# Window attention and two MLPs on one core: products with v of two pairs in one run, v stationary from the third window, and another model of VectorE's hold in the list schedule

## The chip, the core and the metric

The kernel runs on 1 core of one Trainium2 chip. The metric is the device time of one execution in microseconds; the median of 3 runs before the change is 892.06 us (892.01 to 892.25). One further execution was profiled, and the rows below are from it. Engines are TensorE (PE; PEld is its weight load), VectorE (DVE), ScalarE (ACT), GpSimd (POOL) and SyncE (SP), whose queue issues nearly all DMAs.

## The reference

Attention over 4 batches, 8 heads, 576 tokens, head size 64, with a window: heads 0 to 3 see the last 32 tokens, heads 4 to 7 every fourth of the last 128. Then two MLPs on the 2304 tokens of width 512 and inner width 2048.

```python
rel = pos[:, None] - pos[None, :]
mask_plain = (rel >= 0) & (rel < 32)
mask_dil = (rel >= 0) & (rel < 128) & (rel % 4 == 0)
scores = np.where(mask, q @ k.T / np.sqrt(64), -1e9)
attn = np.exp(scores - scores.max(-1)); attn = attn / (attn.sum(-1) + 1e-9)
x = (attn @ v)                                   # heads side by side: 2304 x 512
h = x @ w_in1; x = np.maximum(0.01 * h, h) @ w_out1
h = x @ w_in2; out = (np.maximum(h, 0) + np.log1p(np.exp(-abs(h)))) @ w_out2
```

## The kernel before, in words

**Attention.** The tokens are cut into 8 windows of 288 (half a batch each; `w` is 0 to 7). In each window four pairs of heads (`p` 0 to 3) are worked on: pairs 0 and 1 are plain, pairs 2 and 3 dilated. For a pair TensorE forms scores with keys on the partitions and queries along the free axis (L661 for dilated pairs, L674 for plain ones, from the third window on), VectorE adds the mask (L682, L689), GpSimd takes the maximum over the partitions (`rowmax`, L699, a `partition_all_reduce`), VectorE subtracts it (L703), ScalarE takes the exponential (L706). What comes then has two forms.

- *Scores stationary* (`pv`, L724): the exponentials are the stationary operand, v with a column of ones moves. Each row's sum comes out as column 65; ScalarE and VectorE make the reciprocal and scale (`inv_sum`, `inv`: L734, L740, L741), and TensorE transposes the result (`xT`, L750). A dilated pair has its products in two halves, each with a PSUM bank of its own.
- *v stationary* ("turned"; `pv_late`, L760): v is the stationary operand, 64 columns wide, one half of the array's columns for each of the two heads; the exponentials move, and the result is transposed already. The sums come from a second `partition_all_reduce` on GpSimd (`sums`, L768); VectorE spreads them by transposes (`spread`, L776), adds 1e-9, takes reciprocals and transposes back (`recip`, L781 to L784), and scales (`norm`, L788).

In both forms ScalarE rounds the result to a high part (`x_hi`, L807) and VectorE subtracts for the low part (`x_lo`, L811). These go into one of two rooms for x, and are what the first MLP's products read; each pair makes a quarter of the width of x. Before the change a pair is turned if `w >= 3 and (dilated or p == 0 or w > 3)`: 19 pairs.

**First MLP.** Eight blocks of tokens (256, 256, 352 and then 288 wide), 16 slices of the inner width each: 12 products for h (L833), then on ScalarE and VectorE the activation and its split in two parts (L849, L854, L858), then 12 products into y (L876). These main products fill TensorE; attention for later windows runs between them. VectorE and ScalarE also turn the weights of both MLPs from their raw words into high and low parts (L321 to L381).

**Second MLP.** It starts when the last block is done, from about 500 us on, and has no attention beside it (L1017, L1078, L1090).

**What sets the order.** All work is written as operations with an engine, an estimated cost, dependences, buffers that it takes and gives back, and a due time. `run_schedule` simulates the engines on these costs, takes at each step the ready operation with the earliest due time, and puts out the program in that order. On the chip every engine runs its instructions in that order, and waits only for data and buffers. Due times go back from each block's first product: the last low part of pair `p` is due `11 * (3 - p)` us ahead of that of pair 3 (`STAG`). Buffers that matter here: 2 score tiles (`s`), 1 tile for maxima and sums (`mx`), 2 tiles for reciprocals (`xn`), 2 PSUM banks for attention (`at`), 2 tiles each for k, q and v.

The schedule also models that VectorE runs slower or not at all while GpSimd runs a `partition_all_reduce`. An operation with a `lock` has its simulated end put off; one with a small `lock` is also ranked 6 us later (`WAIT`) while the hold lasts. Before the change the hold lasts for the whole GpSimd operation from 75 us on, and the VectorE operation goes on at 0.33 or 0.7 of its speed; ahead of 75 us it lasts 1.2 us and stops it.

Of the kernel before, what the change touches and what calls it, by code (L numbers as in the profile page):

```python
# [11 lines left out]
F32 = mybir.dt.float32  # L12
# [14 lines left out]
def kernel(  # L27
# [58 lines left out]
    TURN = 3  # L86
# [7 lines left out]
    class Op:  # L94
        def __init__(self, eng, cost, fn, *args, deps=(), order=(), acq=(), rel=(),
                     target=None, margin=0.0, start=0.0, lib=None, slack=0.0, lock=0.0, optional=False, hold=0.0, lead=None, shy=False):
# [11 lines left out]
    def run_schedule(slots):  # L108
# [64 lines left out]
        running = {}  # L173

        def slowed(start, work, rate):
            beside = locked - start
            return start + (work / rate if work <= rate * beside else beside + work - rate * beside)

# [5 lines left out]
        while True:  # L184
# [17 lines left out]
            for e in engines:  # L202
# [3 lines left out]
                for o in pools[e]:  # L206
                    if ready_at[o] <= now + 1e-9 and all(free[a] >= o.acq.count(a) for a in o.acq):
                        rank = (ready_at[o] if e == "bw" else o.prio) + (HOLD if switch(o) else 0.0) + (WAIT if 0.0 < o.lock < 0.5 and now < locked else 0.0), o.n
# [26 lines left out]
                if best.lib == "reduce":  # L235
                    locked = best.end if now > LOCK_FROM else now + LOCKED
                    beside = running.get("dve")
                    if now > LOCK_FROM and beside is not None and beside.lock and beside.end > now:
                        beside.end = slowed(now, beside.end - now, beside.lock)
                        busy["dve"] = beside.end - TRAIL["dve"]  # L240
                        heapq.heappush(events, beside.end)
                        heapq.heappush(events, busy["dve"])
                if best.lock and now < locked:
                    best.end = slowed(now, best.cost, best.lock) if now > LOCK_FROM else locked + best.cost
                running[e] = best
# [239 lines left out]
    class Pair:  # L485
        def __init__(self, w, p):
# [8 lines left out]
            self.turned = w >= TURN and (self.dil or p == 0 or w > TURN)  # L495
# [258 lines left out]
        def pv_late(self):  # L754
            m, kn = self.m, self.kn
            self.xn = att.tile([P, T1], F32, tag="xn", name="xn")
# [15 lines left out]

# [39 lines left out]


# [324 lines left out]
    NSPIN, LOCKED, LOCK, LOCK_FROM, SLACK0, SLACK, HOLDS = 150, 1.2, 0.33, 75.0, 0.3, 1.0, 1.5  # L1138
    LOCKT = 0.7
# [53 lines left out]
    for w in range(NW):  # L1193
# [3 lines left out]
        for p in range(NPAIR):  # L1197
# [58 lines left out]
            else:  # L1256
                nk = a.s0 + T1 - a.klo
                tk = Op("dve", dve(nk) if not dil or a.first else 2 * dve(nk), a.trans_k, deps=[lk] + old_kq, rel=["kr"], lock=LOCKT, **m)
                tq = [Op("dve", (1.0 if turned else 1.2) if dil else 0.48, a.trans_q, deps=[lq] + (old_kq if dil else []),
                         rel=["qr"] if dil else [], lock=LOCKT, **m)]  # L1260
# [56 lines left out]
            for b in blocks:  # L1317
                xready.setdefault(b, []).append(xl)
# [310 lines left out]
```

## Time and profile before

| | |
|---|---|
| median of 3 runs | 892.06 us |
| profiled execution | 890.93 us, its span 889.1 us |
| TensorE busy | 878.9 us, 99% of the span |
| VectorE busy | 654.1 us, 74% |
| ScalarE busy | 399.1 us, 45% |
| GpSimd busy | 146.8 us, 17% |
| maxima of 24 pairs (L699) | mean 2.08 us |
| sums of 19 pairs (L768) | mean 3.74 us |

Busy time of TensorE is the union of its products, whose ends are modelled: products are pipelined, so what one costs is read from the distance of the starts. Time in the rows is counted from the start of the span.

### The profile page before, as it was taken

The page shows a single profiled execution, that of the slowest core. Times are in us where ns is not written, and L with a number is a line of the kernel's source. Part 1 is how long each engine was busy: PE and PEld are TensorE (multiplying, and loading weights), DVE is VectorE, ACT ScalarE, POOL GpSimd, SP SyncE. Part 2 cuts the span into 40 slices and gives each one's busy share as a digit, 9 for nine tenths or more (in the row PEclk, how much of TensorE's full clock was granted, in tenths as well). Part 3 has the DMA queues.
Part 4 walks back from the last instruction along what each step waited for, and adds up shares of the span by engine and source line. Part 5 has one row for each costly group of instructions (what it writes and reads, how often), then busy time and mean ns, then how long its engine had stood idle before and what let it go on. Part 6 is the DMA issues. An engine that isn't in the chain of part 4 may idle for free.

```text
span 889.1 us, 16856 instructions
## 1 busy us (share of the span) xinstructions
PE 878.9 (99%) x6621; PEld 822.2 (92%) x6621; DVE 654.1 (74%) x1166; ACT 399.1 (45%) x780; POOL 146.8 (17%) x71
## 2 busy tenths in 40 slices
PE   9989999999999999999999999999999999999998
PEld 6889999999999999999999999989888898888886
DVE  5999986897897887978944766857765775576553
ACT  5878765345444443444445644324322432243231
POOL 6500120332452433435400000000000000000000
PEclk9999999999999999999999999999999999999999
DMA  9887235664644626435259578333533443334332
GB/s 236 240 261 261 49 83 190 173 180 144 168 123 135 167 65 181 99 107 153 77 167 304 149 227 252 116 101 114 163 122 97 142 146 109 102 112 149 95 95 96
DMA packets 150736, 132.19 MB, mean 149 GB/s; under 512 B 92480, under 2 KB 131200, under 8 KB 150656
## 3 DMA queue, kind: packets, MB, share of 16 engines
q1 hardware_dynamic: 149632, 129.96, 49.1%
q10 hardware_dynamic: 1024, 1.15, 0.5%
q8 instruction: 52, 0.85, 0.4%
q14 instruction: 28, 0.23, 0.1%
HBM read 104.86 MB, written 26.21 MB: 147 GB/s over the span
## 4 chain that ended last, share of the span: by engine, by line
PE 94%; DMA 2%; DVE 2%; ACT 1%; issue 1%; SPq 0%; DVEq 0%; ACTq 0%
PE yp L876 23%; PE yo L1090 23%; PE h L833 23%; PE h L1017 18%; PE hp L1078 3%; DMA raw<-in_moe_w_out_dram 2%; PE pv L760 1%; PE sc L661 1%; PE sc L674 1%; PE pv L724 1%; DVE cf L330 0%; DVE w L381 0%; PE xt L750 0%; DVE cf L339 0%; DVE xn L741 0%
## 5 line engine op out<-in xcount | busy, mean ns | idle before, releaser
L876 PE MATMUL yp<-gh,w 128*128 128x288 f32 (+2 forms) x1024 | 229.1, 299 | 0.0
L833 PE MATMUL h<-xh,w 128*128 128x288 f32 (+2 forms) x1024 | 226.7, 297 | 0.0
L1090 PE MATMUL yo<-wo,w 128*128 128x512 f32 x864 | 222.8, 395 | 0.0
L1017 PEld LDWEIGHTS h<-tr,w 128*128 128x128 f32 x1344 | 174.3, 188 | 11.1
L1090 PEld LDWEIGHTS yo<-wo,w 128*128 128x128 f32 x864 | 152.5, 188 | 27.1
L1017 PE MATMUL h<-tr,w 128*128 128x256 f32 x1344 | 176.7, 279 | 0.0
L876 PEld LDWEIGHTS yp<-gh,w 128*128 128x128 f32 x1024 | 171.3, 188 | 1.9
L833 PEld LDWEIGHTS h<-xh,w 128*128 128x128 f32 x1024 | 171.1, 188 | 1.1
L833 PE MATMUL h<-xl,w 128*128 128x288 f32 (+2 forms) x512 | 151.2, 295 | 0.4 <-DVE xl L811 0.4
L876 PE MATMUL yp<-gl,w 128*128 128x288 f32 (+2 forms) x512 | 150.9, 295 | 0.0
L1055 ACT ACTIVATE ex<-ex 128x512 f32<-128x512 f32 x72 | 45.5, 632 | 159.9 <-DVE ex L1052 158.4
L849 ACT ACTIVATE hc<-h 128x288 f32<-128x288 f32 (+2 forms) x128 | 52.0, 406 | 118.2 <-PE h L833 112.5
L833 PEld LDWEIGHTS h<-xl,w 128*128 128x128 f32 x512 | 96.2, 188 | 0.9 <-DVE xl L811 0.9
L876 PEld LDWEIGHTS yp<-gl,w 128*128 128x128 f32 x512 | 96.2, 188 | 0.1
L858 DVE TENSOR_TENSOR gl<-hc,gh 128x288 fp32r<-128x288 f32 (+2 forms) x128 | 73.9, 578 | 28.7 <-ACT gh L854 27.8
L699 POOL PARTITION_ALL_REDUCE mx<-s x24 | 50.0, 2083 | 243.1 <-DVE s L682 186.8
L768 POOL PARTITION_ALL_REDUCE sm<-s x19 | 71.1, 3740 | 31.8 <-ACT s L706 27.5
L1058 DVE SCALAR_TENSOR_TENSOR ex<-hs,ex 128x512 f32<-128x512 f32 x64 | 44.3, 692 | 35.9 <-ACT ex L1055 35.6
L1063 ACT ACTIVATE w<-ex 128x512 fp32r<-128x512 f32 x72 | 45.3, 629 | 32.8 <-DVE ex L1058 32.8
L321 ACT ACTIVATE cf<-raw 128x512 f32<-128x512 f32 (+1 forms) x48 | 39.9, 830 | 40.7 <-DMA raw<-in_moe_w_out_dram 15.4
L854 ACT ACTIVATE gh<-hc 128x288 fp32r<-128x288 f32 (+2 forms) x128 | 56.6, 442 | 2.9
L1067 DVE TENSOR_TENSOR w<-ex,w 128x512 fp32r<-128x512 f32 x72 | 49.7, 691 | 10.9 <-ACT w L1063 6.2
(113 smaller groups left out, 966.6 us busy)
## 6 DMA issues: line engine op xcount, KB each, us to landing
wo<-w2o SPq DMA_DIRECT2D x80, 512.0 KB, 3.6
raw<-in_moe_w_in_dram SPq DMA_DIRECT2D x32, 512.0 KB, 6.5
raw<-in_moe_w_out_dram SPq DMA_DIRECT2D x32, 512.0 KB, 4.2
w2o<-cf SPq DMA_DIRECT2D x16, 512.0 KB, 3.1
w2a<-cf SPq DMA_DIRECT2D x8, 512.0 KB, 2.6
w2s<-cs SPq DMA_DIRECT2D x8, 512.0 KB
w<-w2a SPq DMA_DIRECT2D x8, 512.0 KB
out_dram<-o SPq DMA_DIRECT2D x28, 128.0 KB, 3.0
```

Source lines behind the costliest of these rows:

```text
L699: nc.gpsimd.partition_all_reduce(self.mx, self.sf, channels=P, reduce_op=bass_isa.ReduceOp.max)
L768: nc.gpsimd.partition_all_reduce(self.sm, self.sf, channels=P, reduce_op=bass_isa.ReduceOp.add)
L833: nc.tensor.matmul(out=h, lhsT=a[:, c, :], rhs=b_[:, c, :], start=(c == 0 and a is whi and b_ is xh), stop=(c == NC - 1 and a is wlo))
L849: nc.scalar.activation(out=hc, in_=hbank.pop(s), func=AF.Prelu, alpha=0.01)
L854: nc.scalar.activation(out=gh, in_=hcopy[s], func=AF.Copy)
L858: eng.tensor_sub(out=gl, in0=hcopy.pop(s), in1=gparts[s][0].bitcast(F32))
L876: nc.tensor.matmul(out=ybank[e][:, o:o + n], lhsT=a[:, e * P:(e + 1) * P], rhs=b_, start=(f == 0 and n == unit_len[u] and a is whi and b_ ...
L1017: nc.tensor.matmul(out=bank[m, b][:, half], lhsT=w[:, a, kb * P:(kb + 1) * P], rhs=t[:, b_, kb], start=(kb == 0 and a + b_ == 0), stop=(kb ...
L1055: nc.scalar.activation(out=self.ex, in_=self.ex, func=AF.Softplus)
L1063: nc.scalar.activation(out=self.gh, in_=self.ex, func=AF.Copy)
L1067: nc.vector.tensor_sub(out=self.gl, in0=self.ex, in1=self.gh.bitcast(F32))
L1090: nc.tensor.matmul(out=obank[c, t], lhsT=a, rhs=b_, start=(opens and n == 0), stop=(closes and n == 2))
```

## The change

- `TURN` goes from 3 to 2, and the rule to `w >= TURN and (dilated or w > TURN)`: the two dilated pairs of the third window and the second plain pair of the fourth become turned, 22 in all.
- Two turned pairs (p 0 and 1, or 2 and 3) share one run on TensorE, `pv_two`. It depends on both pairs' reciprocals and v, takes both `at` banks, and gives both score tiles back at its end. The scalings, `x_hi` and `x_lo` of both pairs come behind it. `xn` is taken at the spreading of the sums, no longer ahead of the products.
- In the schedule's model, a `lock` is now yes or no. A GpSimd reduction holds VectorE for 1.2 us from its start if its cost is under 3 us (a maximum), else for 2.45 us (a sum); a VectorE operation with a lock that starts in that time ends at the hold's end plus its own cost. The transposes (`trans_k`, `trans_q`, `spread`) have no lock any more.

```diff
-    TURN = 3
+    TURN = 2
...
-            self.turned = w >= TURN and (self.dil or p == 0 or w > TURN)
+            self.turned = w >= TURN and (self.dil or w > TURN)
...
                 if best.lib == "reduce":
-                    locked = best.end if now > LOCK_FROM else now + LOCKED
-                    beside = running.get("dve")
-                    if now > LOCK_FROM and beside is not None and beside.lock and beside.end > now:
-                        beside.end = slowed(now, beside.end - now, beside.lock)
...
+                    locked = now + (LOCKED if best.cost < 3.0 else LOCKEDS)
                 if best.lock and now < locked:
-                    best.end = slowed(now, best.cost, best.lock) if now > LOCK_FROM else locked + best.cost
+                    best.end = locked + best.cost
...
+    def pv_two(a, b):
+        a.pv_late()
+        b.pv_late()
...
             if turned:
-                pv = a.o_pv = Op("pe", 0.84, a.pv_late, deps=x + [lv],
-                                 order=[prev(1, "o_pv")], acq=["at", "xn"], **ms)
                 sm = Op("pool", 3.6, a.sums, deps=x, acq=[tag_mx], lib="reduce", **m)
-                t = Op("dve", 2 * dve(288), a.spread, deps=[sm, pv], rel=[tag_mx, tag_s], lock=LOCKT, **m)
-                t = Op("dve", 0.9, a.recip, deps=[t], acq=["rd"], rel=["rd"], lock=LOCKT, **m)
-                xt = Op("dve", dve(288, True), a.norm, deps=[t], rel=["at"], hold=HOLDS, **m)
+                t = Op("dve", 2 * dve(288), a.spread, deps=[sm], acq=["xn"], rel=[tag_mx], **m)
+                t = Op("dve", 0.9, a.recip, deps=[t], acq=["rd"], rel=["rd"], lock=True, **m)
+                a.late, a.lands, xt = t, lv, None
+                if p % 2:
+                    b_ = pairs[-1]
+                    a.o_pv = b_.o_pv = Op("pe", 2 * 0.84 - 0.3, pv_two, b_, a, deps=[t, b_.late, lv, b_.lands],
+                                          order=[pairs[-2].o_pv], acq=["at", "at"], rel=[tag_s, tag_s], **ms)
+                    xt = [Op("dve", dve(288, True), c_.norm, deps=[a.o_pv], rel=["at"], hold=HOLDS, **m) for c_ in (b_, a)]
...
+            for c_, xt_ in ([(a, xt)] if not turned else zip((pairs[-1], a), xt) if p % 2 else ()):
...
+                xh = c_.o_xh = Op("act", act(288, not turned), c_.x_hi, deps=[xt_], order=[pairs[at_ - 1].o_xh if at_ else None],
...
+                xl = Op("dve", dve(288, not turned), c_.x_lo, deps=[xh], rel=[c_.room(c_.p)[1] if not turned else "xn"], lock=turned,
+                        target=tau(first_slot) - 0.5 - stag * (NPAIR - 1 - c_.p), **m)
```

## Rows read from the trace of the kernel before

**Rows 1.** Busy time by stretches: start:end, length, then each engine; PEclk is the granted clock
```profile
58.00:880.00 822.00, 822.00 (x5974) 775.22 (x5973) 606.99 (x1085) 355.89 (x688) 121.06 (x43) 1.00 0.48 143
85.00:210.00 125.00, 125.00 (x1008) 122.79 (x1007) 106.44 (x188) 68.56 (x136) 28.71 (x11) 1.00 0.48 130
210.00:450.00 240.00, 240.00 (x1952) 233.73 (x1951) 200.17 (x364) 104.97 (x222) 92.35 (x32) 1.00 0.47 130
880.00:889.10 9.10, 4.85 (x21) 3.56 (x19) 1.38 (x2) 1.20 (x2) 0.00 (x0) 1.00 0.32 116
```

**Rows 2.** Timeline of TensorE (start, length, instruction, count): a dilated pair, v stationary
```profile
312.92 0.29 PE L833 MATMUL h<-xh,w 128*128 128x288 f32 x1
313.15 0.72 PE L760 MATMUL pv<-s,v 104*64 104x72 f32 x16
...
314.04 0.30 PE L876 MATMUL yp<-gl,w 128*128 128x288 f32 x1
314.17 0.30 PE L876 MATMUL yp<-gh,w 128*128 128x288 f32 x1
```

**Rows 3.** The same: a plain pair, v stationary
```profile
301.50 0.29 PE L833 MATMUL h<-xh,w 128*128 128x288 f32 x1
301.72 0.72 PE L760 MATMUL pv<-s,v 128*64 128x96 f32 x12
...
302.60 0.29 PE L876 MATMUL yp<-gl,w 128*128 128x288 f32 x1
```

**Rows 4.** The same: a dilated pair, scores stationary, and its transposes
```profile
119.72 0.28 PE L876 MATMUL yp<-gh,w 128*128 128x256 f32 x1
119.83 1.20 PE L724 MATMUL pv<-v,s 104*72 104x65 f32 x16
...
121.04 0.28 PE L833 MATMUL h<-xl,w 128*128 128x256 f32 x1
...
126.03 0.28 PE L833 MATMUL h<-xh,w 128*128 128x256 f32 x1
126.15 0.41 PE L750 MATMUL xt<-ident,xn 72*128 72x72 f32 x4
...
126.57 0.28 PE L876 MATMUL yp<-gl,w 128*128 128x256 f32 x1
126.69 0.28 PE L876 MATMUL yp<-gh,w 128*128 128x256 f32 x1
```

**Rows 5.** The same: a plain pair, scores stationary
```profile
109.00 0.28 PE L876 MATMUL yp<-gh,w 128*128 128x256 f32 x1
109.12 1.15 PE L724 MATMUL pv<-v,s 128*96 128x65 f32 x12
...
110.28 0.28 PE L833 MATMUL h<-xl,w 128*128 128x256 f32 x1
```

**Rows 6.** Groups of TensorE by shape: count, busy us, mean ns of one
```profile
L760 PE MATMUL pv<-s,v 104*64 104x72 f32 x160 | 7.2, 232 | 0.0
```

**Rows 7.** Timeline of GpSimd: a sum
```profile
164.68 3.60 POOL L768 PARTITION_ALL_REDUCE sm<-s  x1 [2.11 <-ACT s L706]
```

**Rows 8.** Groups of VectorE by line, 85 to 450 us: count, busy us, mean ns
```profile
L776 DVE STREAM_TRANSPOSE xn<-sm 64x288 f32<-64x288 f32 x38 | 17.8, 468 | 2.4 <-POOL sm L768 2.2
L781 DVE TENSOR_SCALAR rd<-xn 128x9 f32<-128x9 f32 x19 | 11.1, 585 | 0.0
L784 DVE STREAM_TRANSPOSE xn<-rd 128x288 f32<-128x288 f32 x19 | 9.1, 478 | 0.6
```

**Rows 9.** Timeline of VectorE: the same shift, alone and beside that sum
```profile
128.91 0.42 DVE L326 TENSOR_SCALAR cp<-cf 128x512 uint32<-128x512 uint32 x1
...
164.80 2.69 DVE L326 TENSOR_SCALAR cp<-cf 128x512 uint32<-128x512 uint32 x1
```

**Rows 10.** Timeline of VectorE: the last low part ahead of the fifth block
```profile
272.65 0.70 DVE L811 TENSOR_TENSOR xl<-xn,xh 128x288 fp32r<-128x288 f32 x1 [0.24 <-ACT xh L807]
```

**Rows 11.** Timeline of TensorE: the first product of the fifth block
```profile
273.69 0.29 PE L833 MATMUL h<-xh,w 128*128 128x288 f32 x1
```

More of the change, by code (lines that the diff above doesn't have):

```diff
@@ L95, in __init__ @@
         def __init__(self, eng, cost, fn, *args, deps=(), order=(), acq=(), rel=(),
-                     target=None, margin=0.0, start=0.0, lib=None, slack=0.0, lock=0.0, optional=False, hold=0.0, lead=None, shy=False):
+                     target=None, margin=0.0, start=0.0, lib=None, slack=0.0, lock=False, optional=False, hold=0.0, lead=None, shy=False):
             self.eng, self.cost, self.fn, self.args = eng, cost, fn, args
@@ L171, in begins @@
                 coming[u.eng].append(u)
[L173 to L177, printed above, removed]
         result = []
@@ L207, in run_schedule @@
                     if ready_at[o] <= now + 1e-9 and all(free[a] >= o.acq.count(a) for a in o.acq):
-                        rank = (ready_at[o] if e == "bw" else o.prio) + (HOLD if switch(o) else 0.0) + (WAIT if 0.0 < o.lock < 0.5 and now < locked else 0.0), o.n
+                        rank = (ready_at[o] if e == "bw" else o.prio) + (HOLD if switch(o) else 0.0) + (WAIT if o.lock and now < locked else 0.0), o.n
                         if best is None or rank < best_rank:
@@ L771, in spread @@
         def spread(self):
+            self.xn = att.tile([P, T1], F32, tag="xn", name="xn")
             src = self.sm.rearrange("p (t j m) -> p t j m", t=self.nt, j=2)
@@ L1257 @@
                 nk = a.s0 + T1 - a.klo
-                tk = Op("dve", dve(nk) if not dil or a.first else 2 * dve(nk), a.trans_k, deps=[lk] + old_kq, rel=["kr"], lock=LOCKT, **m)
+                tk = Op("dve", dve(nk) if not dil or a.first else 2 * dve(nk), a.trans_k, deps=[lk] + old_kq, rel=["kr"], **m)
                 tq = [Op("dve", (1.0 if turned else 1.2) if dil else 0.48, a.trans_q, deps=[lq] + (old_kq if dil else []),
-                         rel=["qr"] if dil else [], lock=LOCKT, **m)]
+                         rel=["qr"] if dil else [], **m)]
             tag_s, tag_mx = ("es", "emx") if early else ("s", "mx")
@@ L1304 @@
                                 rel=[a.room(half if dil else p)[1], "rd"], **m))
-            room = [f"x{u % 2}" for u in rooms] if p == 0 else []
+            rooms_x = [f"x{u % 2}" for u in rooms]
+            room = rooms_x if p == 0 else []
             if not turned:
@@ L1346 @@
         lw = Op("act", act(n), a.low, order=[o], **m)
-        o = Op("dve", dve2(n), a.shift, deps=[o], acq=["cp"], lock=LOCK, **m)
-        o = Op("dve", dve(n), a.join, deps=[o], rel=["cp"], lock=LOCK, **m)
-        o = Op("dve", dve(n), a.add, deps=[o, lw], rel=["raw"] if layer else [], lock=LOCK, **m)
+        o = Op("dve", dve2(n), a.shift, deps=[o], acq=["cp"], lock=True, **m)
+        o = Op("dve", dve(n), a.join, deps=[o], rel=["cp"], lock=True, **m)
+        o = Op("dve", dve(n), a.add, deps=[o, lw], rel=["raw"] if layer else [], lock=True, **m)
         if layer == 0:
             o = Op("act", act(n), a.split_hi, deps=[o], **m)
-            wready[0, f] = Op("dve", dve(n), a.split_lo, deps=[o], rel=["cf"], lock=LOCK, **m)
+            wready[0, f] = Op("dve", dve(n), a.split_lo, deps=[o], rel=["cf"], lock=True, **m)
         else:
```

30 lines of the change are left out of this document (11 added, 19 removed).

## The prediction

> **What bounds the kernel now.** I read the busy time by stretches first. From 58 to 880 us TensorE is busy for all 822.00 us at the full granted clock; only the last 9.1 us, where the result drains, have holes (4.85 busy) [rows 1]. The reader is to see in that table that no other engine fills its stretch: between 85 and 210 us VectorE has 106.44 of 125 us and GpSimd 28.71, and TensorE all of it. So in this region the end moves with TensorE alone: a microsecond of its work that goes is a microsecond off the end, as long as nothing that it needs comes late. Attention for a window of 288 tokens runs between the two products of earlier tokens. Everything that the change touches lies between 85 and 450 us.
>
> **Prices of one run, from the order of TensorE's work.** Then I read the timeline around the attention runs. I take the start of the last main product ahead of a run and the start of the second main product behind it, and subtract two usual steps. What is left is what the run costs. A step is 0.134 us for 288 columns (314.04 to 314.17 [rows 2], rounded there).
> - Dilated pair, v stationary: 314.04 - 312.92 - 0.27 = 0.85 us [rows 2].
> - Plain pair, v stationary: 302.60 - 301.50 - 0.27 = 0.83 [rows 3].
> - Dilated pair, scores stationary (a step of 256 columns: 126.57 to 126.69): products 121.04 - 119.72 - 0.23 = 1.09, transposes behind them 126.57 - 126.03 - 0.23 = 0.31, together 1.40 [rows 4].
> - Plain pair, scores stationary: products 110.28 - 109.00 - 0.23 = 1.05 [rows 5]; its transposes have three instructions where the dilated have four, estimated at 0.28 from those; together 1.33.
>
> How much of the 0.85 is paid per run, and how much per product? Sixteen instructions take 0.72 us [rows 2], the last alone about 0.23 (mean 232 ns [rows 6]), so the step is (0.72 - 0.23) / 15 = 0.033 us and sixteen steps are 0.52. The remaining 0.33 us is at the two edges: the first product starts 0.23 us behind the last main one instead of 0.13, and the rest is lost behind the run. The run with scores stationary has hardly any edge: (1.20 - 0.23) / 15 is 0.065, sixteen steps are 1.03 of a cost of 1.09 [rows 4]. That run is also two pieces of the program, one for each half of the pair on a PSUM bank of its own, so pieces in a row need not pay at their joint. The edge belongs to the tile of 64 columns, which is entered and left.
>
> **The change part by part.**
> (1) *Two pairs in one run.* 19 pairs keep v stationary before; after, 22 do: both dilated pairs of the third window and all four pairs of the five windows behind it. They make 11 runs, where each alone would make 22. Each joint saves one edge: 11 x 0.33 = 3.6 us. No row shows two such runs in succession. The bounds are 0 (the second pair's first products start as a run's first do) and 11 x 0.35 = 3.9 (the edge, and the wait of a second entry). I take 0.33, since the two pairs of a run have the same tile shape.
> (2) *Three more pairs with v stationary.* Two dilated: 2 x (1.40 - 0.85) = 1.1 us. One plain, the second of the fourth window: 1.33 - 0.83 = 0.5.
> (3) *What these three add elsewhere.* Three sums on GpSimd at 3.60 us [rows 7], and on VectorE per pair two transposes of 0.47, an addition of 0.585 (mean, holds included) and a transpose of 0.48 [rows 8], some 2 us, in place of the old reciprocals and scalings. Cover: VectorE's 18.6 idle us and GpSimd's 96 in 85 to 210 us [rows 1]. Counted as nothing; with that cover gone it costs at most 3 x 2 us.
> (4) *The products moved behind both reciprocals.* On the chip the run waits for the exponentials, v and two PSUM banks, not for the reciprocals; only its place in TensorE's order moves. What waits behind it: both score tiles (there are two) come free only then, so the next pair's scores come later; and both v tiles, so the next v loads come later, and with them the q, k and weight loads behind them in SP's one queue. The chain of two pairs through the single tile for maxima and sums is some 20 us (estimate: two sums at 3.60, two maxima and the VectorE steps between them). The time for it is 30 us: 210 to 450 us hold 32 GpSimd operations, two for a pair, so 16 pairs in 240 us [rows 1]. Counted as nothing. With that cover gone the next scores would wait for the difference; the PSUM banks themselves are held for a shorter time, as the scaling follows at once.
> (5) *VectorE's hold in the list schedule.* No instruction is added, only the order changes. A sum starts on GpSimd at 164.68 and runs 3.60 us [rows 7]; the shift on VectorE that starts at 164.80 takes 2.69 us to 167.49, where the same shape takes 0.42 alone [rows 9]. So it was held until 167.07, 2.4 us into the sum, and then ran at its usual speed while the sum went on. That is the new model's phase of 2.45; the old one slowed such operations to a third over the whole sum. I expect the list's times to come nearer to the chip's. Bounds: no gain is to be had, since no wait is left to remove in 58 to 880 us; the loss through a worse order is in the rivals. Value 0.
> The Trainium skill's page "SBUF — State Buffer", section "Who interferes with whom", says that whoever issues first keeps the shared ports for its whole instruction and the other engine is fully blocked. By it the shift would have ended at 168.28 + 0.42 = 168.70; the trace has 167.49, so it agrees about the blocking and not about its length.
>
> Sum: 3.6 + 1.1 + 0.5 = 5.2 us less on TensorE, all on the path. The profiled execution took 890.93 us (span 889.1 and 1.83 around it), so 885.7. The median of the runs shown is 1.13 above the profiled one: **886.9 us**.
>
> **Rivals.**
> *A. The last pair is late for its block (slower).* Ahead of the fifth block of tokens the last low part of the attention output starts at 272.65 and takes 0.70 [rows 10]; the block's first product starts at 273.69 [rows 11] and needs that part, its last quarter, eight products later, at about 274.8. The lead is 1.4 us. Between the last reciprocal and that low part the new order puts a run of 0.85 + 0.52 = 1.37 us, a second scaling (some 0.45) and a second low part (0.70), with handovers of about 0.24 as in that row some 3.2 us. If pairs start when they start now, TensorE stands 3.2 - 1.4 = 1.8 us; at six windows 10.8, less 5.2, is 5.6 us more: 897.7. It decides from a loss of 0.9 us per window, a last low part 2.3 us nearer to its block. Against it: the shared run takes its due time from its earlier pair, which the schedule places 11 us ahead of the later one, so the later pair's scores, maximum and sum are ranked that much earlier than now. Chance 0.10.
> *B. The joint saves nothing.* For it: no row of two such runs. Then 1.6 us remain: 890.4. Chance 0.06.
> *C. VectorE becomes the bound* early in 85 to 210 us, where it still splits the weights of the first products, with the third window's pairs pulled ahead; TensorE then waits for weights for as long as it gained: about 892. Against it: 18.6 us idle there. Chance 0.05.
> *D. The gain comes, less 1 to 2 us of new waits* in the reshuffled order: about 888.3. For it: VectorE has under a sixth of its time left. Chance 0.12.
> *E. VectorE is held for the whole sum*, so the new list is too early by 3.60 - 2.4 = 1.2 us for a held operation; at two windows with a lead as small as that of the fifth block this is 2.4 us: 889.3. The row of the shift speaks against it. Chance 0.03. (This is the rule of the Trainium skill's page named in part 5.)
>
> **How the numbers follow.** The forecast has 0.64, its own range 886.2 to 887.7 (joints at 0.28 to 0.35, waits of up to half a microsecond). 0.2% of the median is 1.8 us, about what a measurement of this kernel can tell from no change. Faster: the forecast, D and E, 0.79. Same: B and C, 0.11. Slower: A, 0.10. The range goes from 885.8 (joints at 0.35, and handovers of TensorE that shrink a little) to 890.4, which takes in D, E and B and leaves out C and A.
>
> **What would show it.** Right: 11 runs of 24 to 32 instructions at line L760, each costing about 1.35 us by the same subtraction; no transposes at L750 for the third window's dilated pairs and the fourth window; 22 sums on GpSimd; TensorE busy without a hole from 58 to 875 us. A joint at which the second pair's first product starts 0.2 us or more behind the first pair's last shows B. Waits of a block's first product for a low part show A, waits for split weights C. Operations of VectorE begun at a sum's start that end some 2.4 us later plus their own time agree with the new list's phase; ends behind the sum show E. The forecast is wrong if TensorE's holes between 58 and 875 us add up to more than 1 us.

## The result, and the profile after

The changed kernel takes 898.27 us (median of 4 runs, 897.61 to 898.68); the kernel before, beside it, 892.03 (890.93 to 892.25). The ratio is 1.0072 [1.0054, 1.0089]: slower by 6.2 us, where 5.2 us less were forecast. The profiled execution took 898.44 us, its span 896.7. A few executions took some 14 us more than the others of the same kernel; every change of time below leaves them out. Line numbers in a row are those of its own kernel: L823 and L866 here are L833 and L876 of the kernel before, L746 and L754 are L760 and L768.

The busy time by stretches, columns as in [rows 1]; 85 to 147 us is the stretch in which the third window's pairs now have sums:

```profile
58.00:880.00 822.00, 815.55 (x5938) 769.09 (x5937) 608.17 (x1091) 352.73 (x682) 133.40 (x46) 1.00 0.47 142
85.00:147.00 62.00, 60.94 (x548) 59.74 (x548) 57.61 (x93) 38.63 (x71) 17.56 (x6) 1.00 0.28 68
210.00:450.00 240.00, 234.71 (x1918) 227.80 (x1915) 194.78 (x363) 103.14 (x221) 92.45 (x32) 0.99 0.48 132
```
and the same 62 us of the kernel before:
```profile
85.00:147.00 62.00, 62.00 (x558) 61.38 (x557) 52.30 (x93) 38.34 (x75) 9.27 (x4) 1.00 0.35 87
```

TensorE had no hole from 58 to 880 us in [rows 1]; now it has 6.45 us of them, where the prediction took more than 1 us as the sign that it is wrong. And holes are not all: products that run at the lower clock count as busy (rows below). VectorE goes from 52.30 to 57.61 busy us of 62 in the early stretch, so that 4.4 us of it are idle; over 85 to 210 us it still has 14.3 idle (106.44 to 110.67 busy of 125).

The runs on TensorE cost what was forecast. The timeline around one shared run, for [rows 2, 3]:

```profile
331.86 0.29 PE L866 MATMUL yp<-gh,w 128*128 128x288 f32 x1
332.08 1.22 PE L746 MATMUL pv<-s,v 104*64 104x72 f32 x32
333.23 0.40 PE L823 MATMUL h<-xh,w 128*128 128x288 f32 x1
333.47 0.29 PE L823 MATMUL h<-xl,w 128*128 128x288 f32 x1
```

333.47 - 331.86 - 0.27 is 1.34 us for two pairs; the eleven runs lie at 1.33 to 1.35. Summed by the same subtraction, attention's runs cost 47.1 us before and 41.8 after, waits left out: 5.3 less.

The rest is waits. I add up, from 57 to 860 us, by how much each main product starts later behind the one ahead than its usual step, and by how much each attention run costs more than its price: 0.2 us before, 12.0 after. Span against span: 11.8 of waits, less 5.3 of work, plus 0.7 by which the first block's first product starts later (39.84 instead of 39.14 us; run 6, in the same order, has 38.96), is 7.2 of the 7.6 us. The 12.0 us lie in five places: 1.9 at 101 to 109 us, 0.4 near 199.5, 4.6 at the start of the fourth block (214.5 to 222.6), 2.4 a little later (229.8 to 235.6), most of it where that block's first products into y wait for the copies of the third block's y, and 2.8 in four waits for `gl`, the low part that VectorE makes for the products into y.

**The fourth block**, the dearest. TensorE's timeline:

```profile
216.78 0.29 PE L823 MATMUL h<-xh,w 128*128 128x288 f32 x1
219.03 0.40 PE L823 MATMUL h<-xh,w 128*128 128x288 f32 x1 [1.96 <-ACT xh L793]
219.72 0.61 PE L823 MATMUL h<-xl,w 128*128 128x288 f32 x1 [0.29 <-DVE xl L797]
...
221.08 0.49 PE L866 MATMUL yp<-gh,w 128*128 128x352 f32 x1
221.38 0.49 PE L866 MATMUL yp<-gl,w 128*128 128x352 f32 x1
```
ScalarE, VectorE and SP's queue beside it:
```profile
217.74 0.66 ACT L308 ACTIVATE cf<-raw 128x512 f32<-128x512 f32 x1 [3.23 <-DMA w2o<-cf]
218.30 1.28 ACT L793 ACTIVATE xh<-xn 128x288 fp32r<-128x288 f32 x2
...
214.31 0.82 DVE L774 TENSOR_TENSOR xn<-pv,xn 128x288 f32<-128x288 f32 x2
...
219.01 1.27 DVE L797 TENSOR_TENSOR xl<-xn,xh 128x288 fp32r<-128x288 f32 x2 [0.16 <-ACT xh L793]
...
211.14 0.33 SPq L357 DMA_DIRECT2D w2o<-cf  x1
211.56 4.38 SPq L546 DMA_DIRECT2D v<-in_v_dram  x6
```

`x_hi` needs only the scaled output, which VectorE has ready at 215.1 (L774). But ahead of it in ScalarE's order stands the first step of a weight conversion (L308), and that waits for the buffer `cf`, from which a store is still going out. The store is issued at 211.14, with two raw loads ahead of it and six loads of v behind, and its end releases ScalarE at 217.74: 6.6 us. The list has the store issued at 204.57 and landed at 207.07, 5.1 us ahead of the block's first product (212.19 in the list); on the chip it lands 1.7 us behind that product (216.01). Of this change of 6.8 us, 4.1 are the landing and 2.7 that the issue is late against TensorE. The first half of `x_hi` then comes some 2 us late. Behind the stop TensorE has a granted clock of 0.55 over 3.8 us, so the lower of its two levels (1.2 GHz) for most of that stretch, and 352-column products start some 0.3 us apart (221.08, 221.38) where 0.16 is usual:

```profile
215.00:216.70 1.70, 1.70 (x17) 1.54 (x17) 0.72 (x2) 0.00 (x0) 0.00 (x0) 1.00 0.95 307
219.10:222.90 3.80, 3.51 (x13) 3.30 (x14) 3.80 (x8) 1.89 (x5) 0.00 (x0) 0.55 0.34 119
223.00:229.00 6.00, 6.00 (x47) 5.68 (x47) 4.14 (x11) 2.05 (x5) 3.29 (x1) 1.00 0.88 235
```

**The waits for `gl`.** GpSimd, VectorE and TensorE around the first of the four, for [rows 7, 9]:

```profile
268.19 3.70 POOL L754 PARTITION_ALL_REDUCE sm<-s  x1 [3.60 <-ACT s L693]
...
267.75 0.69 DVE L317 SCALAR_TENSOR_TENSOR cf<-cf,cp 128x512 uint32<-128x512 uint32 x1
268.48 2.90 DVE L326 CUSTOM_DVE_ANT_0 cf<-raw,cf 128x1024 uint16<-128x1024 uint16 x1
271.30 0.44 DVE L848 TENSOR_TENSOR gl<-hc,gh 128x288 fp32r<-128x288 f32 x1
...
271.80 0.40 PE L866 MATMUL yp<-gl,w 128*128 128x288 f32 x1 [0.49 <-DVE gl L848]
```

A sum starts at 268.19. The operation begun at 267.75 ends in its usual time (268.44); the next, of a line that takes 0.69 us undisturbed, takes 2.90 to 271.38: 0.69 behind 270.69, which is 2.5 us into the sum. So the phase is as part 5 read it from the shift, and as the new model has it. What the model can't know is on which side of a sum's start an operation falls: in these rows 0.3 us (268.48 against 268.19) make 2.2 us.

### The profile page after: what moved, and what is told of

Same layout as the page of the kernel before. It is cut to its first block, busy times and chain, and to the rows that moved or that the text cites. A ratio compares the mean times of both kernels' runs of the same rounds, so it can differ in the third digit from the quotient of the medians.

```text
span 896.7 us, 16821 instructions
## 1 busy us (share of the span) xinstructions
PE 878.6 (98%) x6610; PEld 821.1 (92%) x6610; DVE 656.5 (73%) x1174; ACT 397.1 (44%) x775; POOL 159.0 (18%) x74
## 4 chain that ended last, share of the span: by engine, by line
PE 55%; POOL 1%; DVE 1%; SPq 1%; DMA 1%; issue 0%; ACT 0%; POOLq 0%
PE yo L1080 22%; PE h L1007 18%; PE yp L866 6%; PE h L823 6%; PE hp L1068 2%; SPq L529 1%; DMA raw<-in_moe_w_in_dram 1%; POOL mx L686 0%; POOL sm L754 0%; PE pv L746 0%; DVE rd L767 0%; PE sc L648 0%; DVE s L676 0%; DVE xn L762 0%; PE sc L661 0%
## 5 line engine op out<-in xcount | busy, mean ns | idle before, releaser
L866 PE MATMUL yp<-gh,w 128*128 128x288 f32 (+2 forms) x1024 | 229.2, 298 | 1.7 <-DVE ys L884 1.1
L823 PE MATMUL h<-xh,w 128*128 128x288 f32 (+2 forms) x1024 | 227.5, 297 | 2.0 <-ACT xh L793 2.0
L866 PEld LDWEIGHTS yp<-gh,w 128*128 128x128 f32 x1024 | 172.2, 188 | 3.9 <-DVE ys L884 1.6
L823 PEld LDWEIGHTS h<-xh,w 128*128 128x128 f32 x1024 | 171.5, 188 | 3.2 <-ACT xh L793 2.2
L866 PE MATMUL yp<-gl,w 128*128 128x288 f32 (+2 forms) x512 | 151.8, 296 | 1.4 <-DVE gl L848 1.3
L823 PE MATMUL h<-xl,w 128*128 128x288 f32 (+2 forms) x512 | 151.6, 296 | 0.7 <-DVE xl L797 0.7
L848 DVE TENSOR_TENSOR gl<-hc,gh 128x288 fp32r<-128x288 f32 (+2 forms) x128 | 76.3, 597 | 35.8 <-ACT gh L844 32.2
L866 PEld LDWEIGHTS yp<-gl,w 128*128 128x128 f32 x512 | 96.5, 188 | 2.7 <-DVE gl L848 2.6
L823 PEld LDWEIGHTS h<-xl,w 128*128 128x128 f32 x512 | 96.4, 188 | 1.4 <-DVE xl L797 1.4
L754 POOL PARTITION_ALL_REDUCE sm<-s x22 | 82.8, 3764 | 46.9 <-ACT s L693 31.7
L308 ACT ACTIVATE cf<-raw 128x512 f32<-128x512 f32 (+1 forms) x48 | 39.8, 829 | 65.1 <-DMA raw<-in_moe_w_in_dram 25.4
L1057 DVE TENSOR_TENSOR w<-ex,w 128x512 fp32r<-128x512 f32 x72 | 49.7, 691 | 10.3 <-ACT w L1053 5.5
```

Source lines behind the costliest of these rows:

```text
L754: nc.gpsimd.partition_all_reduce(self.sm, self.sf, channels=P, reduce_op=bass_isa.ReduceOp.add)
L823: nc.tensor.matmul(out=h, lhsT=a[:, c, :], rhs=b_[:, c, :], start=(c == 0 and a is whi and b_ is xh), stop=(c == NC - 1 and a is wlo))
L848: eng.tensor_sub(out=gl, in0=hcopy.pop(s), in1=gparts[s][0].bitcast(F32))
L866: nc.tensor.matmul(out=ybank[e][:, o:o + n], lhsT=a[:, e * P:(e + 1) * P], rhs=b_, start=(f == 0 and n == unit_len[u] and a is whi and b_ ...
L1057: nc.vector.tensor_sub(out=self.gl, in0=self.ex, in1=self.gh.bitcast(F32))
```

## The experiments

These explanations of the 12 us of waits stood against each other: the new hold model puts out a worse order (H in the expectations); pairing crowds buffers and queues (P); the third window's turn falls on a VectorE that has no room (W); or any order other than that of before meets such waits by chance (N). A further one, that one instruction waits in a queue ahead of the fourth block (Q), came from the rows above; M is the thought that a list whose stores land later is better anywhere.

Each change of the time below is of medians, against the kernel before, run beside it on the same chip. *Work* is what the prices in the prediction take from TensorE; *waits* are counted in that run's profile as above, so in one execution.

| run | change of time, us | ratio, interval | work | waits |
|---|---|---|---|---|
| the kernel after | +6.2 | 1.0072 [1.0054, 1.0089] | -5.2 | 12.0 |
| 1 after, old hold | +6.9 | 1.0070 [1.0045, 1.0094] | -5.2 | 13.5 |
| 2 before, new hold | +3.6 | 1.0038 [1.0023, 1.0053] | 0 | 3.8 |
| 3 after, third window as before | +0.6 | 1.0005 [0.9995, 1.0014] | -3.8 | 5.4 |
| 4 before, three more pairs turned | +3.1 | 1.0036 [1.0023, 1.0049] | -1.6 | 5.2 |
| 5 run 3 with old hold | +3.8 | 1.0048 [1.0031, 1.0065] | -3.8 | 8.7 |
| 6 after, sums replaced by a fill | +0.6 | 1.0003 [0.9993, 1.0013] | -5.2 | 4.9 |
| 7 before, sums replaced by a fill | -0.2 | 0.9988 [0.9971, 1.0005] | 0 | 0.0 |
| 8 run 5 with 18 pairs | +0.3 | 1.0002 [0.9988, 1.0016] | -2.5 | 4.8 |
| 9 before, `MA` 12 | +1.6 | 1.0014 [1.0005, 1.0024] | 0 | 2.5 |
| 10 before, STAG 12 | +1.2 | 1.0006 [0.9997, 1.0016] | 0 | 3.5 |
| 11 run 3, `MG` 6 | +2.1 | 1.0014 [1.0004, 1.0025] | -3.8 | 5.7 |
| 12 run 4, third window's sums a fill | +1.4 | 1.0017 [1.0004, 1.0029] | -1.6 | 3.4 |
| 13 after, store lands 4 us later in the list | +0.8 | 1.0011 [0.9998, 1.0023] | -5.2 | 6.1 |
| 14 run 3 with the same | +3.2 | 1.0029 [1.0017, 1.0042] | -3.8 | 7.5 |
| 15 after, one instruction moved | +5.8 | 1.0067 [1.0049, 1.0086] | -5.2 | 11.2 |
| 16 run 14 with a guard | +13.5 | 1.0152 [1.0134, 1.0170] | -3.8 | 17.3 |
| 17 after, one conversion moved | +3.2 | 1.0031 [1.0018, 1.0044] | -5.2 | 10.3 |
| 18 before, store lands 4 us later in the list | -0.5 | 0.9993 [0.9984, 1.0002] | 0 | 0.9 |

In every row work and waits add up to the change of time within 2.4 us; in two of the rows with the larger gaps, runs 8 and 10, the profiled execution was 3.1 and 1.9 us above the median of its run. Where the interval takes in 1 (runs 3, 6, 7, 8, 10, 13 and 18) the change is not clear of none. Run 7 has the order of before. Run 18 does not: its trace has VectorE's 1166 instructions in another order at some 50 places, from 199 to 400 us, and still has only 0.9 us of waits. All other orders have 2.5 us or more.

Set against their expectations, runs 1, 3, 7, 8 and 11 came out in the range of a theory that they name. Runs 2, 4 and 6 did too, but with other waits than that theory has. Runs 5, 14 and 16 were slower than every range; 9, 10, 12 and 17 fell between two ranges, and 13, 15 and 18 missed the nearest by under 0.2 us.

### Which edit costs it (runs 1 to 4)

1, the old model of the hold put back into the kernel after:

```diff
-                    locked = now + (LOCKED if best.cost < 3.0 else LOCKEDS)
+                    locked = best.end if now > LOCK_FROM else now + LOCKED
...
-                    best.end = locked + best.cost
+                    best.end = slowed(now, best.cost, best.lock) if now > LOCK_FROM else locked + best.cost
```

> The changed kernel with the old model of VectorE's hold in the list (a third of the speed over the whole reduction); pairing and the third window's turn stay. In the profile of the changed kernel TensorE's attention work is 5.3 us less, as forecast, and about 12 us of waits stand against it: 5 us at the fourth block's first product, 2 us at 230 us, 1.9 us at 101 to 108 us, 2.8 us in four waits for a low part of the hidden layer that a sum held on VectorE. Theory H (the new hold model's order is fragile): most waits go, 887 to 889. Theory P (pairing itself crowds the buffers and queues): the waits stay, 896 to 899. Theory W (the third window's turn starts the delay): also 896 to 899.

6.9 us slower, as slow as the change. So the loss does not need the new hold model. The waits lie elsewhere, though; the dearest, with GpSimd and VectorE above it:

```profile
123.61 4.11 POOL L767 PARTITION_ALL_REDUCE sm<-s  x1 [2.56 <-ACT s L706]
...
124.28 2.66 DVE L861 TENSOR_TENSOR gl<-hc,gh 128x256 fp32r<-128x256 f32 x1
126.86 1.41 DVE L326 TENSOR_SCALAR cp<-cf 128x1024 uint32<-128x1024 uint32 x1
128.19 0.94 DVE L775 STREAM_TRANSPOSE xn<-sm 64x288 f32<-64x288 f32 x2
129.16 1.23 DVE L381 TENSOR_TENSOR w<-cf,w 128x1024 fp32r<-128x1024 f32 x1
...
130.44 0.50 PE L836 MATMUL h<-xh,w 128*128 128x256 f32 x2 [2.90 <-DVE w L381]
```

A `gl` falls into the sum of a third-window pair and takes 2.66 us (0.42 alone), and the split of a weight, behind it on VectorE, is late: that is rival C's mechanism, at one place. By the working of the rows above this `gl` was held until 126.94 - 0.42 = 126.52, 2.9 us into a sum that took 4.11 instead of 3.6: beside this longer sum the held part is longer too, and the list has one figure for it.

2, the kernel before with the new model, the inverse edit. 

> The kernel before with the new hold model alone. H: 894 to 898, with waits of TensorE for low parts beside sums. P and W: as before, 891.5 to 892.5, since no run of two and no third window is there.

3.6 us slower without any change of the work: TensorE stops at scores that wait for a PSUM bank which the scaling `xn` has to empty (1.2 us at 111.8, 1.1 at 256.5), not at low parts beside sums as H has it. The edit that was given a value of 0 can cost more than half of the loss; run 5 shows that it can gain as well.

3, the third window's pairs left as before (20 turned pairs, 10 runs):

```diff
-            self.turned = w >= TURN and (self.dil or w > TURN)
+            self.turned = w > TURN
```

> The changed kernel without the third window's turn: all four pairs of the five windows from the fourth on are turned and run in twos, 10 runs, the new hold model. TensorE has 1.1 + 0.33 us more work than in the changed kernel. W: the waits at 101 to 108 us and what follows at the fourth block go, about 890 to 892. H and P: 897 to 900.

0.6 us slower. Turning the third window's two dilated pairs therefore costs 5.6 us net under the new hold model, and 7 us if their 1.4 us of work (1.1 and a joint of 0.3) are put to them; under the old model the same step, from run 5 to run 1, costs 3.1. As `TURN` stays at 2 here, the list's estimates that hang on it (a maximum of the third window at 2.05 instead of 2.2 us, for one) stay those of the change, and the rest of the order moves too; so this is the price of the turn with the order that it brings.

4, the opposite: three more pairs turned in the kernel before, each in its own run.

```diff
-    TURN = 3
+    TURN = 2
...
-            self.turned = w >= TURN and (self.dil or p == 0 or w > TURN)
+            self.turned = w >= TURN and (self.dil or w > TURN)
```

> The kernel before with three more pairs turned (the third window's dilated ones and the fourth's second), each pair in a run of its own, the old hold model. By TensorE's work alone 892.0 - 1.6 = 890.4; that is what H and P expect. W: waits at 100 to 147 us or at the fourth block eat it, 892 to 896.

3.1 us slower, where 1.6 less was the work. So the loss needs neither the shared run nor the new hold model. Its dearest wait:

```profile
203.84 3.61 POOL L768 PARTITION_ALL_REDUCE sm<-s  x1 [1.61 <-ACT s L706]
...
203.90 2.85 DVE L858 TENSOR_TENSOR gl<-hc,gh 128x352 fp32r<-128x352 f32 x1
...
206.81 0.43 PE L876 MATMUL yp<-gl,w 128*128 128x352 f32 x1 [2.07 <-DVE gl L858]
```

The sum starts 0.06 us ahead of a `gl` that TensorE is about to need. It is the last sum of the fourth window, one that the kernel before has as well, and none of the added ones: the new order has moved the `gl` beside it.

### Pairs and sums (runs 5 to 8, 12)

5, run 3 with the old model (edits of 1 and 3 together). 

> Runs of two from the fourth window on (20 pairs, 10 runs), the third window as before, the old hold model. TensorE's work by the prices of the prediction: 10 x 0.33 + 0.5 = 3.8 us less than before. If the third window's turn and the hold model are the two causes of the waits and pairing itself costs nothing: 887 to 888.5. If any new order brings new waits, whatever the part: 890 to 894.

3.8 us slower, against 0.6 with the new model: here the new model helps, where it hurt in run 2 and did nothing clear between run 1 and the kernel after (0.7). The model's effect has no sign of its own. And here pairing, without the third window's turn and without the new model, has met 8.7 us of waits.

6 and 7, the sums replaced in both kernels, with the order as it was:

```diff
-            nc.gpsimd.partition_all_reduce(
-                self.sm, self.sf, channels=P, reduce_op=bass_isa.ReduceOp.add)
+            nc.gpsimd.memset(self.sm, 1.0)
```

> The changed kernel with the 22 sums over the partitions left out: a fill of the same tile on GpSimd stands in their place, so the output is not the reference's. The order of all engines stays, word for word; VectorE is no longer held by the sums, and the sums' own time on GpSimd shrinks. Theory of the holds (VectorE's held operations make what TensorE waits for late): the waits go and the forecast's 5.2 us show, 885.5 to 888. Theory of the queues (ScalarE's and SP's in-order queues stand behind late weight loads): the wait of 5 us at the fourth block stays, 891 to 895.

> The control: the kernel before with its 19 sums left out in the same way. It has no waits of TensorE to remove between 58 and 880 us, so all theories expect no change, 890.5 to 892.

Without sums the order of after is still 0.6 us slower, and that of before gains 0.2, both not clear of no change. The miss to explain is 11.4 us, from the 5.2 less that were forecast to 6.2 more. Sums (their own time and the hold) make some 5.4 of it (6.2 - 0.6, less 0.2); the order of before hides its 19 sums altogether. The rest stays without a single sum: 4.9 us of waits, and among them those at 101 to 109 us and those for the copies at 230 us, which stand in run 6 as in the kernel after. Three of them, in the kernel after and then in run 6:

```profile
104.97 0.47 PE L737 MATMUL xt<-ident,xn 96*128 96x96 f32 x3 [0.51 <-DVE s L669]
109.24 0.76 PE L648 MATMUL sc<-qz,kt 128*128 128x144 f32 x4 [0.48 <-DVE xl L797]
231.91 0.40 PE L866 MATMUL yp<-gh,w 128*128 128x288 f32 x1 [1.10 <-DVE ys L884]
```
```profile
104.37 0.47 PE L737 MATMUL xt<-ident,xn 96*128 96x96 f32 x3 [0.53 <-DVE s L669]
108.64 0.76 PE L648 MATMUL sc<-qz,kt 128*128 128x144 f32 x4 [0.48 <-DVE xl L796]
226.30 0.40 PE L865 MATMUL yp<-gh,w 128*128 128x288 f32 x1 [1.11 <-DVE ys L883]
```

These belong to the order in which VectorE gets its work, not to the sums. At the fourth block the store is issued at 205.76 instead of 211.14, and TensorE does not stop; the four waits for `gl` are gone too. So the late store needs the sums.

12, run 4 with the two sums of the third window replaced:

```diff
+            if self.w == 2:
+                nc.gpsimd.memset(self.sm, 1.0)
+                return
```

> The kernel before with three more pairs turned, each in a run of its own (894.3 as it stood), and in the third window alone the two sums left out (a fill in their place, so the output is not the reference's); order unchanged. If the sums' holds on VectorE in the third window cause the late weights and low parts: 890 to 891.5. If the other VectorE work of the turn or the order does: 893.5 to 895.

1.4 instead of 3.1 us: two sums make some 1.8 us of it, with intervals that overlap. The wait of run 4 beside the fourth window's sum stays (2.1 us).

8, run 5 with `TURN = 3`: 18 pairs in 9 runs. 

> Runs of two with the turn only from the fourth window's dilated pairs on (18 pairs, 9 runs; the fourth window's first pair, turned before, is not), the old hold model. TensorE has 9 x 0.33 - 0.5 = 2.5 us less than before. If pairing is free of waits: 888.5 to 889.5. If any new order brings new waits: 891 to 894.

0.3 us slower, not clear of no change. Its work is 2.5 less, so it too pays 2.8.

### The price of another order (runs 9 to 11)

```diff
-    MA, MC, MC1, MG, MY = 13.0, 0.0, 0.0, 3.0, 5.0
+    MA, MC, MC1, MG, MY = 12.0, 0.0, 0.0, 3.0, 5.0
```

> The kernel before with one planner constant changed: attention is ranked 12 us ahead of its due time instead of 13. No instruction more or less, only another order. Theory N (before's order is one without waits among many; any other order has some): 893 to 896, with 2 to 5 us of waits of TensorE. Theory P+W (the waits come from the run of two and from the third window's turn): 891 to 892.

> The kernel before with the pairs' due times 12 us apart instead of 11; again only another order. N: 893 to 896. P+W: 891 to 892.

A constant of the due times is changed in the kernel before: `MA`, by how many us attention's operations are due ahead of need, from 13 to 12 in 9, and `STAG` from 11 to 12 in 10; the instructions stay. 1.6 and 1.2 us are lost by the medians, the second not clear of no change (ratio 1.0006). In 9 the profile's longest wait is 1.2 us for an `xn`; in 10 runs of attention are dearer by 0.4 to 1.0 us each. So an order can cost 1 to 1.5 us by itself. That any other order does is not shown: run 18 below puts out another one as well and loses nothing.

11, run 3 with `MG`, the same margin for the activation and for the copies of y, at 6 instead of 3. 

> The changed kernel without the third window's turn, and the split of the hidden layer and the copies of y ranked 6 us ahead of their due time instead of 3, since TensorE waited for just these. N, with the cause named as VectorE operations that come late by one hold: waits shrink from 5.4 us to 1 to 3, 888 to 890. If it is chance which order has waits: 890 to 894.

2.1 us, where run 3 had 0.6: more margin for all of them takes no waits away (5.7 us against 5.4).

### The fourth block (runs 13 to 18)

13, 14 and 18 tell the list that the buffer comes free 4 us later, in the kernel after, in run 3 and in the kernel before:

```diff
-                Op("none", 0.0, lambda: None, deps=[w2_stored["o", f]], rel=["cf"])
+                Op("landing", 4.0, lambda: None, deps=[w2_stored["o", f]], rel=["cf"])
```

> The changed kernel with 4 us more for the landing of the weight stores in the list, so that conversions are placed later everywhere. Q: as the swap or better, 892 to 894.5. Otherwise 896 to 899.

> The same without the third window's turn. In the trace without that turn one conversion also stood 3.2 us for a store, and a low part of the hidden layer behind it came late by 1.7 us. Q: 889 to 890.5, against 891.8 without the change of the landing. Otherwise 891 to 893.

> The kernel before, with the list told that the store out of the conversion buffer takes 4 us longer to land; control for the run that did the same to the kernel after. Theory Q (that run gained 6.4 us because it took one named wait away): the kernel before has no such wait, so nothing is to be gained here: 891 to 892.5, and what is lost is the price of another order, 0.5 to 1.5 us as in the two other re-plannings. Theory M (a list whose store lands as late as on the chip is better anywhere): 889 to 890.5.

13 gains 5.4 us on the kernel after (each against its own kernel before; the 6.4 in an expectation sets times of two chips against each other). The conversion is placed behind `x_hi` now, which goes as soon as the scalings are done, and the block's products run without a stop:

```profile
213.56 1.29 ACT L793 ACTIVATE xh<-xn 128x288 fp32r<-128x288 f32 x2 [1.74 <-DVE xn L774]
...
215.76 0.68 ACT L308 ACTIVATE cf<-raw 128x512 f32<-128x512 f32 x1
...
215.55 0.43 PE L823 MATMUL h<-xh,w 128*128 128x288 f32 x2
215.82 0.30 PE L823 MATMUL h<-xl,w 128*128 128x288 f32 x1
```

18 has another order and the same time (-0.5 us, interval 0.9984 to 1.0002), so the longer landing is no gain by itself, and reordering no loss by itself. But 14 loses 2.6 us on run 3: its new order stops 2.4 us at the fourth block, for an `x_hi` again.

15, only the one conversion step (L308) moved behind `x_hi` in the order of after:

```diff
+    at_ = next(i for i, o in enumerate(schedule) if getattr(o.fn, "__name__", "") == "rebias" and o.start > 207.5)
+    to_ = max(i for i, o in enumerate(schedule) if getattr(o.fn, "__name__", "") == "x_hi" and o.fn.__self__.w == 3)
+    schedule.insert(to_, schedule.pop(at_))
```

> The changed kernel with one weight conversion moved behind the high parts of the fourth window's last two pairs in the put-out order; all else as it was. Theory Q (that conversion, waiting for a store, holds up ScalarE's queue and with it the fourth block): the wait of 5 us, with TensorE's half clock behind it, goes, 893 to 894.5. If those pairs are late for another reason: 897 to 898.5.

`x_hi` starts at 213.39 then, but only 0.4 us come back, less than the intervals can tell. The next step of the same piece, the shift, stands ahead of `x_lo` on VectorE and passes the wait on:

```profile
216.85 0.43 DVE L313 TENSOR_SCALAR cp<-cf 128x512 uint32<-128x512 uint32 x1 [2.53 <-ACT cf L308]
217.19 1.22 DVE L797 TENSOR_TENSOR xl<-xn,xh 128x288 fp32r<-128x288 f32 x2
...
217.88 0.40 PE L823 MATMUL h<-xl,w 128*128 128x288 f32 x1 [2.07 <-DVE xl L797]
```

17, all three steps of that piece moved behind `x_lo`, and nothing else:

```diff
+    last = max(i for i, o in enumerate(schedule) if name(o) == "x_lo" and o.fn.__self__.w == 3)
+    to_ = next(i for i in range(last, len(schedule)) if name(schedule[i]) == "join")
+    piece = [next(i for i, o in enumerate(schedule) if name(o) == n and o.start > t)
+             for n, t in (("rebias", 207.5), ("shift", 208.5), ("low", 208.5))]
...
+    schedule[at_:at_ + 1] = moved
```

> The kernel after, with one piece of a weight conversion (its rebias and low part on ScalarE, its shift on VectorE) moved as a whole behind the last x_hi and x_lo of the fourth block, in both queues. Theory Q (the fourth block waits because x_hi and x_lo stand in order behind an instruction that waits for a store to land): the last low part ends before 217 us, the block's wait of 5 us is gone, and so is the half clock behind it: ratio 1.001 to 1.003, 892 to 894 us, near the 891.9 of the run with the longer landing in the list. Theory N (most of that run's gain came from another order as a whole): the gain stays under 2 us, 896 to 898. Whatever comes, the four waits for gl from 271 to 409 us and those at 101 to 108 us stay, since the rest of the order is unchanged.

3.0 us come back. The block starts at 215.31 and its first slice runs through; then the piece, now later, holds up the next pair's scores, which wait for a tile that VectorE has to empty (L669). The piece itself waits for the store as before, 1.07 us on ScalarE and with it 1.24 on VectorE:

```profile
218.77 0.32 PE L866 MATMUL yp<-gh,w 128*128 128x352 f32 x1
220.97 1.27 PE L661 MATMUL sc<-qr,kt 64*128 64x96 f32 x12 [1.88 <-DVE s L669]
...
217.33 0.66 ACT L308 ACTIVATE cf<-raw 128x512 f32<-128x512 f32 x1 [1.07 <-DMA w2o<-cf]
...
218.03 0.43 DVE L313 TENSOR_SCALAR cp<-cf 128x512 uint32<-128x512 uint32 x1 [1.24 <-ACT cf L308]
...
220.47 0.81 DVE L669 TENSOR_TENSOR s<-sc,masksb 128x288 f32<-128x288 f32 x2
```

That costs 2.3 us more than the run's price. So the queue order around one piece is the cause of the block's stop: with the piece behind `x_lo` it is gone. Some two thirds come back and not all, because the piece still waits for the store, now ahead of what the scores need. The four waits for `gl` stay (0.2 to 1.1 us each).

16, run 14 with a guard of 0.5 us in the hold model: an operation that began less than 0.5 us ahead of a reduction counts as held.

```diff
+                    beside = running.get("dve")
+                    if beside is not None and beside.lock and beside.end > now and now - beside.start < 0.5:
+                        beside.end = locked + beside.cost
```

> The kernel of e14 with one more rule in the list: a VectorE operation begun up to 0.5 us ahead of a reduction counts as held too. If the hard edge of the hold model is what is left: 887.5 to 889.5. If chance decides which order has waits: 889 to 893.

The worst of all, 13.5 us slower: 6.5 us of waits for `ys`, the copy of a block's y (5.4 of it at 292.2), and 3.7 for a `gl` at 236.5. A margin that is meant for one risk moves the order to others.

## Why the prediction was wrong

**What bounds the kernel** held: TensorE sets the end, and work and waits on it add up to the time in all 18 runs, within 2.4 us. Its condition, "as long as nothing that it needs comes late", is what failed. The row of 822.00 busy us was read as room for late deliveries, where it says only that this one order had no wait.

**(1) and (2)** were right: 1.33 to 1.35 us a shared run against 1.35 worked out, no transposes for the turned windows, 5.3 us less on TensorE against 5.2. Rival B is out.

**(3)**, "counted as nothing", is the first step that failed. The cover of 18.6 idle us was taken over 125 us; the third window's two sums fall into its first half. There VectorE had 9.7 us idle and now 4.4 of 62; operations that take over 0.1 us longer than the usual one of their line while a reduction runs went from 2 (0.5 us lost) to 7 (5.2 us), half of that beside the two sums and half beside maxima. Run 3 against the kernel after puts 5.6 us net on those two pairs, run 1 against run 5 3.1; run 4 against its work, with the fourth window's plain pair, 4.7; run 12 gives 1.8 of that to the sums themselves. The bound given, 3 x 2 us if the cover was gone, stood in no rival. That it is of the right size is partly luck: it counts VectorE's added steps, where the rows show holds and a late order.

**(4)**, "counted as nothing", failed as well, and without (3): run 5, with the products moved and paired, the third window as before and the old hold model, was to gain 3.8 us and met 8.7 us of waits, run 8 4.8. It failed not as it was weighed. The dearest wait in the kernel after is set neither by the chain of 20 us nor by the v loads: a conversion step that waits for a landing of 6.6 us stands ahead of `x_hi` at one block. Runs 13, 15 and 17 show that wait and what it costs; run 6 shows that it needs the sums. Which of run 5's waits the moved products make, and which the order around them, no run tells apart. The queues were looked at for what the products do to them, not for what the new list would put ahead of what they feed.

**(5)** had the right phase (2.5 us in the row of 268.48) and the wrong inference. That "the list's times come nearer to the chip's" did not make the order better: 3.6 us worse in run 2, 3.2 better from run 5 to run 3, 0.7 better, not clear of none, from run 1 to the kernel after. Rival E is out: held for the whole sum, the operation begun at 268.48 would have ended at 271.89 + 0.69 = 272.58, and it ended at 271.38. Rival E's rule is that of the Trainium skill's page "SBUF — State Buffer", section "Who interferes with whom", which states a lock for the whole instruction where VectorE runs in a 2-port mode (no row shows whether it does here). The trace agrees about the blocking and not about its length, and the measurement decides.

**Rival A** named 897.7 us, 0.6 off, by luck, since its mechanism is another: the longer tail of the last pair ahead of every block, at six windows. Only the fourth block's last two quarters come late, and not by that tail. **Rival C**'s waits for split weights are seen in run 1 alone. **Rival D** was the right kind with the wrong size, 1 to 2 us of new waits where 12 came. Its price was never worked out: run 9 shows that an order changed by one constant can lose 1.6 us (run 10 1.2, run 18 none), and runs 2, 3 and 5 that a larger change of the list meets 4 to 9 us of waits. About half of the miss of 11.4 us is of this kind, as it stays in run 6 without any sum.

**What stays open.** About 4 of the 12 us (101 to 109 us, and the copies at 230 us) are not made by sums, as run 6 keeps them; which edit puts VectorE's work in that order has no experiment of its own. Nor does any run show what makes that one store take 6.6 us to land. And which orders happen to be good is not explained: run 14 gains the landing and loses 2.6 us, run 11 more margin and 1.5. The chance in the order is of the size of the differences between runs 3, 8 and 13, which I don't rank. No version with the change was faster than the kernel before.

## What to carry to other kernels

Where a profile shows the bounding engine without a hole for 800 us, the order that gave it is part of the tuning: work removed from that engine pays only by what the new order's waits leave over, so price the reordering itself before the work, by changing a few harmless constants (here +1.6, +1.2 and -0.5 us: a single one would have misled). Look for cover in the stretch where the added work falls, not over a mean, and for each in-order queue ask what the new list puts ahead of the instruction that the bounding engine waits for, above all one that waits for a store to land.

## What the runs showed of the hardware that was not expected

A stop of about 2 us can cost more than itself: at the fourth block 2.1 us of standing are followed by 3.8 us at a granted clock of 0.55, with starts at nearly twice the usual distance, some 1.2 us on top. It need not: behind run 14's stop (2.25 us idle by the profile, where the fourth block's has 1.96) and run 17's (1.88) the granted clock stayed at 1.00, the upper level (2.4 GHz). Their stretches behind the stop:

```profile
218.50:222.50 4.00, 3.55 (x25) 2.88 (x26) 1.29 (x2) 3.35 (x8) 0.00 (x0) 1.00 1.05 370
220.97:224.00 3.03, 3.02 (x25) 2.86 (x26) 3.03 (x6) 0.99 (x3) 2.19 (x1) 1.00 0.67 110
```

And a sum on GpSimd that takes 3.6 to 3.7 us later on took 4.83 and 4.00 us (L754, from 115.42 and 125.28 us) in the stretch in which VectorE was busy for 57.61 of 62 us; that the busy VectorE is the cause is not shown.
